# Output tiles in turn over four buffers and scaled x over six, in a linear-attention and FFN kernel

## The chip, the cores and the metric

The kernel runs on one core of a Trainium2 chip. The metric is the device time of one execution in microseconds (us); the lower, the better. A core has five engines that this text names as the profile does: PE (matrix multiplication, with its weight loads, PEld, beside it), DVE (VectorE), ACT (ScalarE), POOL (GpSimd) and SP (SyncE, which here only issues transfers). They run side by side, each in the order of its own instructions, and wait for each other through semaphores.

## The reference

Eight batches, eight heads, 576 tokens, head size 64. Every row of q and k is mapped to 256 positive features, and the attention is linear: keys and values are summed first, and each query is multiplied with the sum.

```python
def phi(x):
    proj = np.einsum('bhsd,df->bhsf', x, w_phi)                  # 64 -> 128
    proj = proj - np.max(np.abs(proj), axis=-1, keepdims=True)
    return np.concatenate([np.exp(proj), np.exp(-proj)], axis=-1)
q_p, k_p = phi(q), phi(k)
kv = np.einsum('bhsf,bhsd->bhfd', k_p, v)
num = np.einsum('bhsf,bhfd->bhsd', q_p, kv)
den = np.einsum('bhsf,bhf->bhs', q_p, np.sum(k_p, axis=2))[..., None] + 1e-06
x = (num / den)                      # reordered to 4608 tokens x 512
out = (np.maximum(x @ w_gate, 0.0) * (x @ w_val)) @ w_out        # 512 -> 1536 -> 512
```

The outputs are 4608 x 512 numbers in float32.

## The kernel before

**Stages.** For a batch, k and q are loaded, turned (so that the head dimension lies along the partitions) and multiplied with w_phi; DVE takes the largest absolute value of each row (`row_max`, L319), ACT the exponentials (L368, L565), POOL scales v (L328). PE sums keys and values (L486, L509), a copy takes the sums out of PSUM (L422), and PE multiplies them with the queries (L595). DVE joins the two halves of the features (L614, L626), takes the reciprocal of the denominator (L633), and POOL multiplies with it (L635): the result is `xu`, 128 tokens of scaled x in bf16. In the first two batches (`TURN = 2`) PE turns `xu` (L648 to L657); from then on, and for the chunks that hold the last 64 tokens of two batches, SP issues a transposing transfer `xT<-xu` (L643). The flag `by_dma` says which of the two holds for a chunk.

**FFN.** `ffn(g)` is called for nine groups of 512 tokens: eight batches, and a ninth with the remaining tokens of all batches. A group has twelve steps of gate and value products (L725, four matmuls each), a copy of the value product (L740), a joint relu and product into `h2` (L747), and then four output tiles of 128 tokens: twelve matmuls (L773, three thirds of four) into one PSUM bank `po`, a copy of it by ACT or DVE into an SBUF tile `out_sb` (L787), and a transfer of 256 KB to HBM which SP issues (`store`, L754; the last group stores in two halves, one issued by SP and one by ACT, L758).

**Order.** `ORDER` (L26) is a list of 1427 numbered steps, written out by hand, that says in which order the steps of all batches and groups are issued; a prime at a number gives a copy to the other engine. Nothing reorders them later: each engine runs its instructions, and SP and POOL issue their transfers, in that order.

**Buffers.** A tile of a pool takes the next buffer of its name. Before an instruction may write a buffer again, it waits until all that read the buffer's tile before has ended, a transfer's landing included. So `out_sb`, with two buffers, waits for the landing of the store of the tile two before it, and `xu`, with three, for the transposing transfer of the tile three before it:

```python
x["xu"] = sb_f.tile([P, H, D], BF16, name="xu")                     # L634, pool sb_f: 3 buffers
out_sb = sb_g.tile([P, DM], FP32, name="out_sb", bufs=2)            # L785
```

PSUM has eight banks, taken in turn by all products (`bank()`, L176). PE may write a bank again when the copy or reduction that read it has ended, so a late copy of `po` holds up whatever PE writes eight banks later.

The q and k of the first two batches are turned by PE and copied into tiles `tT4` (1 KB a partition, three buffers) and `tT8` (2 KB a partition, two buffers) of the pool `sb_T` (`turned_copy`, L282). From batch 2 on a transfer turns them and these five buffers are not used any more.

Of the kernel before, what the change touches and what calls it, by code (L numbers as in the profile page):

```python
# [8 lines left out]
FP32 = mybir.dt.float32  # L9
BF16 = mybir.dt.bfloat16  # L10
# [5 lines left out]
TURN = 2  # L16
# [103 lines left out]
def kernel(  # L120
# [21 lines left out]
    B, H, S, D = q.shape  # L142
    F = w_phi.shape[1]
    DFF = moe_w_gate.shape[1]
    DM = out.shape[1]
    P = 128
# [373 lines left out]

    GROUPS = ((0, 3), (3, 3), (6, 2))

    def q_item(key, groups, T, chunks, by_dma, blocks=None):


# [57 lines left out]
        for ci, (batches, place, col, dst, xkey) in enumerate(chunks):  # L583
            x = xs[ci]
            np_ = P // len(batches)
            for j, (lo, n) in enumerate(GROUPS):

                @atoms.add("n", *key, ci, j)
                def _(alt, x=x, j=j, lo=lo, n=n, batches=batches, place=place):
                    for bi, b in enumerate(batches):  # L590
                        pn = x["pn", j, bi] = bank()
                        for i in range(n):
                            slot, blk = place(lo + i)
                            for s in range(2):
                                nc.tensor.matmul(  # L595
                                    pn[:, E * (2 * i + s) : E * (2 * i + s + 1)],
                                    lhsT=x["qp"][:, s, slot, blk, :],
                                    rhs=kv_of(b, lo + i)[:, s, :],
                                )

                def halves(x, j, lo, n, batches, np_=np_):
                    for bi in range(len(batches)):
                        rows = slice(np_ * bi, np_ * (bi + 1))
                        ab = x["pn", j, bi][:, 0 : 2 * E * n].rearrange(
                            "p (c s e) -> p c s e", s=2, e=E
                        )
                        yield rows, ab[rows]

                @atoms.add("nt", *key, ci, j)
                def _(alt, x=x, j=j, lo=lo, n=n, batches=batches, col=col, np_=np_, halves=halves):  # L610
                    x["t", j] = sb_s.tile([P, 3, E], FP32, name="t", bufs=4)
                    for rows, ab in halves(x, j, lo, n, batches):
                        c = st["c"][rows, col(lo) : col(lo + n - 1) + 1 : col(1) - col(0)]
                        nc.vector.tensor_tensor(  # L614
                            x["t", j][rows, 0:n],
                            ab[:, :, 1],
                            c[:, :, None].to_broadcast([np_, n, E]),
                            op=ALU.mult,
                        )

                @atoms.add("nu", *key, ci, j)
                def _(alt, x=x, j=j, lo=lo, n=n, batches=batches, halves=halves):
                    if "u" not in x:
                        x["u"] = sb_f.tile([P, H, E], FP32, name="u")
                    for rows, ab in halves(x, j, lo, n, batches):
                        nc.vector.tensor_tensor(  # L626
                            x["u"][rows, lo : lo + n], ab[:, :, 0], x["t", j][rows, 0:n], op=ALU.add
                        )

            @atoms.add("xu", *key, ci)  # L630
            def _(alt, x=x):
                x["r"] = sb_s.tile([P, H, 1], FP32, name="r")
                nc.vector.reciprocal(x["r"], x["u"][:, :, D : D + 1])  # L633
                x["xu"] = sb_f.tile([P, H, D], BF16, name="xu")  # L634
                copy_of(alt, nc.gpsimd, nc.vector).tensor_tensor(  # L635
                    x["xu"], x["u"][:, :, 0:D], x["r"].to_broadcast([P, H, D]), op=ALU.mult
                )

            if by_dma:

                @atoms.add("xd", *xkey)
                def _(alt, x=x, dst=dst):
                    nc.sync.dma_start_transpose(out=dst(), in_=x["xu"].rearrange("p h d -> p (h d)"))  # L643

            else:

                @atoms.add("xT", *xkey)
                def _(alt, x=x):  # L648
                    x["pt"] = turn_on_pe(
                        [x["xu"][:, 2 * i : 2 * i + 2].rearrange("p a d -> p (a d)") for i in range(NDC)]  # L650
                    )

                @atoms.add("xc", *xkey)
                def _(alt, x=x, dst=dst):
                    copy_by(copy_of(alt, "DVE", "ACT"))(
                        dst(), x["pt"][:, 0 : NDC * P].rearrange("p (a b) -> p a b", b=P)
                    )  # L657
# [55 lines left out]
            q_tails(b // 2)  # L713


    def ffn(g):
        st = {}
        steps = [(fi, 0, SF) for fi in range(NFC)]
        if g == 0:
            steps = [(fi, P * lo, P * hi) for lo, hi, f0, f1 in FIRST for fi in range(f0, f1)]  # L720

        def half_step(fi, w, lo, hi):
            ps = bank()[:, 0 : hi - lo]
            for dc in range(NDC):
                nc.tensor.matmul(  # L725
                    ps,
                    lhsT=w[:, dc, P * fi : P * fi + P],
                    rhs=xTs[g][:, dc, lo:hi],
                    start=(dc == 0),
                    stop=(dc == NDC - 1),  # L730
                )
            return ps

        for n, (fi, lo, hi) in enumerate(steps):

            @atoms.add("fv", g, n)
            def _(alt, n=n, fi=fi, lo=lo, hi=hi):
                ps = half_step(fi, wv_sb, lo, hi)
                st["val", n] = sb_g.tile([P, SF], BF16, name="val_sb")[:, 0 : hi - lo]
                copy_by(copy_of(alt, "ACT", "DVE"))(st["val", n], ps)  # L740

            @atoms.add("fg", g, n)
            def _(alt, n=n, fi=fi, lo=lo, hi=hi):
                if "h2" not in st:
                    st["h2"] = sb_h.tile([P, NFC, SF], BF16, name="h2")
                ps = half_step(fi, wg_sb, lo, hi)
                nc.vector.scalar_tensor_tensor(  # L747
                    st["h2"][:, fi, lo:hi], ps, 0.0, st["val", n], op0=ALU.max, op1=ALU.mult
                )

        def store(t, out_sb, c0, c1):
            if g < B:
                rows = out[S * g : S * g + SF, c0:c1].rearrange("(p c) n -> c p n", c=C)
                nc.sync.dma_start(out=rows[t], in_=out_sb)  # L754
                return
            for half, eng in enumerate((nc.sync, nc.scalar)):
                r0 = S * (2 * t + half) + SF
                eng.dma_start(  # L758
                    out=out[r0 : r0 + SM, c0:c1], in_=out_sb[SM * half : SM * (half + 1), :]
                )  # L760

        for t in range(4):
            cols = LAST if g == B and t == 3 else ((0, DM),)
            for part, (c0, c1) in enumerate(cols):
                for third in range(3):

                    @atoms.add("fo", g, t, part, third)
                    def _(alt, t=t, part=part, third=third, c0=c0, c1=c1):
                        if third == 0:
                            st["po", t, part] = bank()[:, 0 : c1 - c0]  # L770
                        po = st["po", t, part]
                        for fi in range(4 * third, 4 * third + 4):
                            nc.tensor.matmul(  # L773
                                po,
                                lhsT=st["h2"][:, fi, P * t : P * t + P],
                                rhs=wo_sb[:, fi, c0:c1],
                                start=(fi == 0),
                                stop=(fi == NFC - 1),
                            )
                        if third < 2:  # L780
                            return
                        if part:
                            out_sb = sb_f.tile([P, H, E], FP32, name="u").rearrange("p h e -> p (h e)")
                        else:
                            out_sb = sb_g.tile([P, DM], FP32, name="out_sb", bufs=2)  # L785
                        out_sb = out_sb[:, 0 : c1 - c0]
                        copy_by(copy_of(alt, "ACT", "DVE"))(out_sb, po)  # L787
                        store(t, out_sb, c0, c1)

    for g in range(B + 1):  # L790
        ffn(g)
# [54 lines left out]
```

## Time and profile before

| | us |
|---|---|
| Median of 3 runs | 379.87 |
| The runs | 379.75, 379.87, 386.1 |
| The profiled execution: its own time | 382.8 |
| Its span, first to last instruction | 380.8 |
| PE busy in the span | 365.3 (96%) |
| DVE busy | 290.4 (76%) |
| ACT busy | 213.6 (56%) |
| POOL busy | 151.2 (40%) |

The profiled execution took 2.0 us more than its span, which is what lies around the first and the last instruction, and 2.9 us more than the median. TensorE's granted clock was full in all 40 slices. Times within the execution are counted from the start of the span. A row of the timeline gives start, duration, engine, line, operation, tiles and count, and in brackets how long the engine stood idle before and what ended that.

### The profile page before, as it was taken

How to read it: one execution, taken by the hardware profiler on the slowest of the kernel's cores; microseconds unless marked ns; L12 is line 12 of the kernel's file. 1: busy time of each engine (PE TensorE's matmuls, PEld its weight loads, DVE VectorE, ACT ScalarE, POOL GpSimd, SP SyncE). 2: the span in 40 equal slices, each digit the busy share in tenths (PEclk: the TensorE clock that was granted, in tenths of full speed). 3: DMA queues.
4: the chain of work that ended last, by engine and by line, in shares of the span. 5: the costliest groups of instructions: out<-in, count | busy, mean ns of one | idle time of the engine just before them, and what ended most of it. 6: DMA issues, size and time to landing. Idle time of an engine off the chain costs nothing.

```text
span 380.8 us, 8916 instructions
## 1 busy us (share of the span) xinstructions
PE 365.3 (96%) x3452; PEld 196.8 (52%) x3502; DVE 290.4 (76%) x633; ACT 213.6 (56%) x509; POOL 151.2 (40%) x201
## 2 busy tenths in 40 slices
PE   7789999898999999999989999999999999999996
PEld 4467455445555545464545544465455444444443
DVE  6998989797886789888858886988768927834641
ACT  6997888776776556885864549882750212111101
POOL 5882663359265283911752035933710220010000
PEclk9999999999999999999999999999999999999999
DMA  8999999999199959880378768720410131011003
GB/s 258 204 200 218 228 143 143 199 239 118 36 208 228 161 87 167 164 183 14 72 126 197 108 162 126 144 16 16 109 58 2 28 87 53 3 53 71 2 0 110
DMA packets 87929, 45.10 MB, mean 118 GB/s; under 512 B 55824, under 2 KB 82000, under 8 KB 87888
## 3 DMA queue, kind: packets, MB, share of 16 engines
q1 hardware_dynamic: 60208, 30.42, 36.4%
q0 software_dynamic: 27200, 13.57, 28.2%
q10 hardware_dynamic: 480, 0.56, 0.5%
q8 instruction: 27, 0.44, 0.5%
q14 instruction: 14, 0.11, 0.1%
HBM read 37.78 MB, written 9.44 MB: 124 GB/s over the span
## 4 chain that ended last, share of the span: by engine, by line
PE 79%; ACT 8%; DMA 5%; POOL 2%; issue 2%; DVE 1%; SPq 1%; another core or an unknown queue 0%; DVEq 0%; POOLq 0%
PE pa L725 44%; PE pa L773 20%; PE pa L595 4%; PE pa L312 4%; PE pa L486 3%; ACT kp L368 3%; ACT qp L565 3%; DMA vn<-in_v_dram 3%; DMA out_dram<-out_sb 2%; PE pa L547 2%; POOL vs L328 1%; SPq L292 1%; PE pa L509 1%; PE pa L271 1%; DMA vn<-in_k_dram 1%
## 5 line engine op out<-in xcount | busy, mean ns | idle before, releaser
L725 PE MATMUL pa<-xT,wv_sb 128*128 128x512 bf16 (+1 forms) x384 | 97.9, 370 | 0.9
L725 PE MATMUL pa<-xT,wg_sb 128*128 128x512 bf16 (+1 forms) x385 | 98.0, 370 | 0.8
L773 PE MATMUL pa<-wo_sb,h 128*128 128x512 bf16 (+2 forms) x427 | 97.6, 373 | 1.1 <-issue 0.3
L747 DVE SCALAR_TENSOR_TENSOR h<-pa,val_sb 128x512 bf16<-128x512 f32 (+1 forms) x112 | 74.6, 669 | 26.8 <-PE pa L725 20.7
L740 ACT CAST val_sb<-pa 128x512 bf16<-128x512 f32 (+1 forms) x67 | 38.1, 575 | 97.9 <-PE pa L725 88.8
L635 POOL TENSOR_TENSOR xu<-u,r 128x512 bf16<-128x512 f32 x36 | 37.3, 1041 | 139.3 <-DVE r L633 69.7
L565 ACT ACTIVATE qp<-pa 128x512 bf16<-128x512 f32 x144 | 76.2, 616 | 14.4 <-PE pa L547 14.1
L368 ACT ACTIVATE kp<-pa 128x512 bf16<-128x512 f32 (+1 forms) x152 | 77.6, 603 | 11.8 <-PE pa L312 10.4
L328 POOL TENSOR_TENSOR vs<-vn,ek 128x512 bf16<-128x512 f32 (+1 forms) x68 | 67.4, 1004 | 34.4 <-DMA vn<-in_v_dram 18.0
L725 PEld LDWEIGHTS <-wv_sb 128*128 128x128 bf16 x448 | 41.8, 98 | 45.0 <-issue 1.2
L725 PEld LDWEIGHTS <-wg_sb 128*128 128x128 bf16 x448 | 41.6, 98 | 43.4 <-issue 0.5
L773 PEld LDWEIGHTS <-h 128*128 128x128 bf16 x444 | 40.8, 98 | 44.6 <-issue 0.8
L319 DVE TENSOR_REDUCE mq<-pa 128x4 f32<-128x512 f32 x72 | 46.5, 683 | 11.1 <-PE pa L312 11.0
L319 DVE TENSOR_REDUCE mk<-pa 128x4 f32<-128x512 f32 (+1 forms) x76 | 47.8, 654 | 3.9 <-ACT kp L368 2.3
L626 DVE TENSOR_TENSOR u<-pa,t 128x195 f32<-128x195 f32 (+3 forms) x120 | 38.1, 333 | 3.3
L614 DVE TENSOR_TENSOR t<-pa,cq 128x195 f32<-128x195 f32 (+3 forms) x120 | 36.9, 326 | 2.5 <-PE pa L595 1.3
L787 DVE COPY out_sb<-pa 128x512 f32<-128x512 f32 x21 | 14.5, 688 | 28.8 <-PE pa L773 20.3
L595 PEld LDWEIGHTS <-qp 128*128 128x128 bf16 x640 | 28.1, 98 | 14.2 <-ACT qp L565 0.9
L740 DVE CAST val_sb<-pa 128x512 bf16<-128x512 f32 (+1 forms) x45 | 30.7, 682 | 4.4 <-PE pa L725 3.0
L595 PE MATMUL pa<-kv,qp 128*128 128x65 bf16 x640 | 31.1, 193 | 1.1 <-ACT qp L565 0.5
L787 ACT COPY out_sb<-pa 128x512 f32<-128x512 f32 (+1 forms) x15 | 8.9, 594 | 23.5 <-PE pa L773 18.7
L486 PEld LDWEIGHTS <-kp 128*128 128x128 bf16 x480 | 16.7, 97 | 5.9 <-issue 1.5
(68 smaller groups left out, 262.7 us busy)
## 6 DMA issues: line engine op xcount, KB each, us to landing
out_dram<-out_sb SPq DMA_DIRECT2D x32, 256.0 KB, 2.9
vn<-in_v_dram SPq DMA_DIRECT2D x6, 1024.0 KB, 7.1
qn<-in_q_dram POOLq DMA_DIRECT2D x8, 512.0 KB, 8.5
kn<-in_k_dram POOLq DMA_DIRECT2D x6, 512.0 KB, 8.6
wv_sb<-in_moe_w_val_dram POOLq DMA_DIRECT2D x3, 512.0 KB, 10.4
wg_sb<-in_moe_w_gate_dram POOLq DMA_DIRECT2D x3, 512.0 KB, 9.1
wo_sb<-in_moe_w_out_dram POOLq DMA_DIRECT2D x1, 1536.0 KB, 19.9
vn<-in_v_dram SPq DMA_DIRECT2D x1, 1152.0 KB, 11.7
```

The source lines that it names most:

```text
L319: nc.vector.tensor_reduce(m, some.rearrange("p (c f) -> p c f", f=F), axis=AX.X, op=ALU.max, apply_absolute_value=True,)
L328: eng.tensor_tensor(dst[:, :, s, 0:D], src, ek[:, :, s : s + 1].to_broadcast(list(src.shape)), op=ALU.mult,)
L368: nc.scalar.activation(st["kp"][:, s, 0 : n // 2, par, :], st["banks"][par][:, 0 : n // 2 * F].rearrange("p (a f) -> p a f", f=F), AF.Exp, ...
L565: nc.scalar.activation(x["qp"][:, s, slot].rearrange("p a b -> p (a b)"), st["cols", i][par], AF.Exp, scale=sign,)
L595: nc.tensor.matmul(pn[:, E * (2 * i + s) : E * (2 * i + s + 1)], lhsT=x["qp"][:, s, slot, blk, :], rhs=kv_of(b, lo + i)[:, s, :],)
L614: nc.vector.tensor_tensor(x["t", j][rows, 0:n], ab[:, :, 1], c[:, :, None].to_broadcast([np_, n, E]), op=ALU.mult,)
L626: nc.vector.tensor_tensor(x["u"][rows, lo : lo + n], ab[:, :, 0], x["t", j][rows, 0:n], op=ALU.add)
L635: copy_of(alt, nc.gpsimd, nc.vector).tensor_tensor(x["xu"], x["u"][:, :, 0:D], x["r"].to_broadcast([P, H, D]), op=ALU.mult)
L725: nc.tensor.matmul(ps, lhsT=w[:, dc, P * fi : P * fi + P], rhs=xTs[g][:, dc, lo:hi], start=(dc == 0), stop=(dc == NDC - 1),)
L740: copy_by(copy_of(alt, "ACT", "DVE"))(st["val", n], ps)
L747: nc.vector.scalar_tensor_tensor(st["h2"][:, fi, lo:hi], ps, 0.0, st["val", n], op0=ALU.max, op1=ALU.mult)
L773: nc.tensor.matmul(po, lhsT=st["h2"][:, fi, P * t : P * t + P], rhs=wo_sb[:, fi, c0:c1], start=(fi == 0), stop=(fi == NFC - 1),)
```

## The change

The five buffers of `tT4` and `tT8` are used again once they are free.

- From group 2 on, every second output tile is a `tT8` tile read as float32, the others stay `out_sb`. The sizes are equal (2 KB a partition). The tiles take four buffers in turn, so a copy waits for the store of the tile four before it. Groups 0 and 1 keep the two buffers (`g < TURN`), and so does the small last piece, which goes into a tile named `u`.
- Of the scaled x that a transfer turns, every second tile is a `tT4` tile (1 KB a partition, as before), the others stay `xu`. That makes six buffers; a multiplication waits for the transposing transfer of the tile six before it.
- `ORDER` and all else are the same: no instruction, transfer or engine is added, removed or moved, no pool grows, and only the buffers and the waits that follow from them differ.

```diff
+    x_count = [0]
+
     def q_item(key, groups, T, chunks, by_dma, blocks=None):
...
-                x["xu"] = sb_f.tile([P, H, D], BF16, name="xu")
+                if by_dma and x_count[0] % 2:
+                    x["xu"] = sb_T.tile([P, 4, P], BF16, name="tT4", bufs=3)
+                    x["xu"] = x["xu"].rearrange("p a (b d) -> p (a b) d", d=D)
+                else:
+                    x["xu"] = sb_f.tile([P, H, D], BF16, name="xu")
+                x_count[0] += by_dma
                 copy_of(alt, nc.gpsimd, nc.vector).tensor_tensor(
...
+    t_count = [0]
+
     def ffn(g):
...
+        def out_tile():
+            if g < TURN or t_count[0] % 2:
+                t = sb_g.tile([P, DM], FP32, name="out_sb", bufs=2)
+            else:
+                t = sb_T.tile([P, 8, P], BF16, name="tT8", bufs=2)
+                t = t.rearrange("p a b -> p (a b)").bitcast(FP32)
+            t_count[0] += 1
+            return t
...
                         else:
-                            out_sb = sb_g.tile([P, DM], FP32, name="out_sb", bufs=2)
+                            out_sb = out_tile()
```

The names of the tiles and of the semaphores tell what is different on an engine. On DVE, in group 3 (batch 3's outputs, at 194 to 201 us of the profile), the two copies of output tiles stand ahead of three row maxima. In the rows the words behind "waits" are semaphores: PE and DVE of those engines' own progress, DMAHW0 to DMAHW7 of eight lanes on which transfers report their landing in turn. Before:

```order
L422 CAST kv_4002<-pa_3981 128x260 [waits PE_49]
L787 COPY out_sb_4008<-pa_3945 128x512 [waits DMAHW2_49,DMAHW3_49,DMAHW1_49,DMAHW7_49,DMAHW0_49,PE_49]
L787 COPY out_sb_4029<-pa_4011 128x512 [waits DMAHW3_49,DVE_49,PE_49]
L319 TENSOR_REDUCE mq16_3849<-pa_4059 128x4 [waits PE_49]
L319 TENSOR_REDUCE mq16_3849<-pa_4060 128x4 [waits PE_49]
L319 TENSOR_REDUCE mq8_4081<-pa_4072 128x4 [waits PE_49]
L422 CAST kv_4116<-pa_4095 128x260 [waits PE_49]
```

The same place of DVE in the change:

```order
L422 CAST kv_4002<-pa_3981 128x260 [waits PE_49]
L805 COPY tT8_4008<-pa_3945 128x512 [waits DMAHW7_49,PE_49]
L805 COPY out_sb_4029<-pa_4011 128x512 [waits DMAHW2_49,DMAHW1_49,PE_49]
L319 TENSOR_REDUCE mq16_3849<-pa_4059 128x4 [waits PE_49]
L319 TENSOR_REDUCE mq16_3849<-pa_4060 128x4 [waits PE_49]
L319 TENSOR_REDUCE mq8_4081<-pa_4072 128x4 [waits PE_49]
L422 CAST kv_4116<-pa_4095 128x260 [waits PE_49]
```

Nothing moved. Before, the copy into `out_sb_4029` waits on lane 3 for the store of the tile `out_sb_3940`, two tiles back; in the change it waits on lane 1 for the store of `out_sb_3299`, four tiles back, and on lane 2 for a load of v that stood earlier on SP. On PE, at the same place, the next sums of keys and values follow eight banks after `pa_4011`, in before as in the change:

```order
L547 MATMUL pa_4085<-qT1_3131,w2_100 128x512 [waits Activation_49]
L547 LDWEIGHTS w2_100
L547 MATMUL pa_4086<-qT1_3131,w2_100 128x512 [waits Activation_49]
L486 LDWEIGHTS kp_3886 [waits DVE_49]
L486 MATMUL pa_4095<-vs_4083,kp_3886 128x65 [waits Pool_49]
```

The weight load of `kp_3886` carries the wait for the bank: it may go when DVE has ended its copy into `out_sb_4029`, which empties `pa_4011`.

## The prediction

> **What bounds the kernel now.** I read the page first (busy times, then the chain that ended last), then the windows from 100 us on, where the new buffers come into use, then the waits of every engine there, and last the timeline around the waits that the buffers cause.
>
> ```profile
> PE 365.3 (96%) x3452; PEld 196.8 (52%) x3502; DVE 290.4 (76%) x633; ACT 213.6 (56%) x509; POOL 151.2 (40%) x201
> PE 79%; ACT 8%; DMA 5%; POOL 2%; issue 2%; DVE 1%; SPq 1%; another core or an unknown queue 0%; DVEq 0%; POOLq 0%
> 100.00:199.67 99.67, 97.83 (x973) 52.62 (x985) 80.42 (x181) 66.87 (x157) 51.97 (x65) 1.00 0.77 137
> 199.67:377.10 177.43, 176.06 (x1308) 88.74 (x1332) 122.83 (x255) 66.09 (x149) 39.47 (x48) 1.00 0.32 70
> ```
>
> The first two rows say that PE is the bound: busy for 96% of the span, and 79% of the last chain. The last two are windows: length, then the busy time of PE, PEld, DVE, ACT and POOL. From 100 us to the last matmul PE stands idle for 99.67 - 97.83 = 1.84 us and 177.43 - 176.06 = 1.37 us, together 3.2 us. The change acts only in this part: groups 0 and 1 keep their two buffers, and where the windows begin the first scaled x is made that a transfer turns. Whatever a wait costs DVE, ACT, POOL or SP, the end moves only by what PE idles for it. So 3.2 us is the most that a removed wait can give, unless PE's work itself became shorter, and no instruction of PE is touched. Matmuls of this size run at their pace: the chain of waits has
>
> ```profile
> 302.92 0.86 PE pa L773 x4
> 330.48 5.18 PE pa L725 x24
> ```
>
> that is 0.86 / 4 = 0.215 and 5.18 / 24 = 0.216 us for one, at a granted clock of 1.00.
>
> **Which of the waits that go were waited for.** The list of waits (total, times, longest) over the whole span has these that bear on the buffers:
>
> ```profile
> DVE out_sb L787 <- DMA out_dram<-out_sb: 8.2, 3, 3.4
> POOL xu L635 <- DVE r L633: 69.7, 15, 17.8
> POOL xu L635 <- issue: 45.3, 5, 26.7
> PE pa L486 <- DVE out_sb L787: 0.9, 1, 0.9
> PE pa L271 <- DVE out_sb L787: 1.1, 1, 1.1
> ```
>
> Three copies of an output tile waited for a store, for 8.2 us in all; PE idled for such a copy twice. The timeline of DVE and PE shows the three, with what PE did about the second:
>
> ```profile
> 69.90 0.69 DVE L787 COPY out_sb<-pa 128x512 f32<-128x512 f32 x1 [1.73 <-DMA out_dram<-out_sb]
> 70.65 0.38 PE L271 MATMUL pa<-ident,xu 128*128 128x128 bf16 x4 [1.09 <-DVE out_sb L787]
> ...
> 191.73 8.24 SPq L754 DMA_DIRECT2D out_dram<-out_sb  x3
> 193.96 3.40 PE L773 MATMUL pa<-wo_sb,h 128*128 128x512 bf16 x15
> 195.48 0.25 POOL L414 CAST vs<-ek 128x16 bf16<-128x16 f32 x1
> 198.35 0.38 PE L547 MATMUL pa<-qT,w 64*128 64x512 bf16 x2
> 198.92 0.69 DVE L787 COPY out_sb<-pa 128x512 f32<-128x512 f32 x1 [3.43 <-DMA out_dram<-out_sb]
> 199.67 0.29 PE L486 MATMUL pa<-vs,kp 128*128 128x65 bf16 x4 [0.94 <-DVE out_sb L787]
> ...
> 312.52 0.69 DVE L787 COPY out_sb<-pa 128x512 f32<-128x512 f32 x1 [3.04 <-DMA out_dram<-out_sb]
> ```
>
> The chain of waits has at the second and the third:
>
> ```profile
> 191.73 7.07 DMA out_dram<-out_sb
> ...
> 304.33 7.23 PE pa L773 x33
> 311.61 2.32 PE pa L773 x10
> ```
>
> The first belongs to group 0, which the change leaves as it is (the 1.1 us of PE with it). At the third PE goes on without a pause: its matmuls run, by the last two rows, from 304.33 to 311.56 and from 311.61 to 313.93, and the copy came while the next tile was being added up. So that wait is worth nothing to PE, nor would the copy have come much sooner, since the matmuls of its own tile lie in the same stretch. There remains the second, in group 3.
>
> **The wait at 198.9 us, worked out.** The tile's twelve matmuls are the last of the 15 shown (one record of 16 is missing) and end at 193.96 + 3.40 = 197.36. The copy started only at 198.92, because the store of the tile two before it, issued at 191.73, landed at 198.80: the chain has it for 7.07 us. With four buffers the copy waits for the store of group 2's last tile, which was issued before the value and gate products of group 3, and starts when PE is done, at about 197.4. With its 0.69 us it ends at about 198.1 instead of 199.61. Behind it on DVE stand three row maxima and a copy of key-value sums, and behind it on SP the tile's own store; all may come up to 1.5 us sooner. PE's next product needs the bank that this copy empties. PE was done with what stands before that at 198.35 + 0.38 = 198.73, and the scaled v that it needs as well was ready at 195.48 + 0.25 = 195.73. So it starts at 198.73 instead of 199.67: 0.94 us of PE, not the 3.43 us of DVE and not the 7.07 us that the chain books on the store, because PE had work under the rest.
>
> What is late next? PE's following products need banks and data of DVE and ACT:
>
> ```profile
> 198.76 1.09 ACT L565 ACTIVATE qp<-pa 128x512 bf16<-128x512 f32 x2 [0.39 <-PE pa L547]
> 199.53 1.88 DVE L319 TENSOR_REDUCE mq<-pa 128x4 f32<-128x512 f32 x3
> 200.42 1.02 PE L725 MATMUL pa<-xT,wv_sb 128*128 128x512 bf16 x3
> 202.15 0.73 PE L595 MATMUL pa<-kv,qp 128*128 128x65 bf16 x18
> ```
>
> The value product at 200.42 writes the bank that the first row maximum empties; it would come at 199.48, and the maximum, 1.88 / 3 = 0.63 us long, can start behind the earlier copy and end by about 199.0. The products at 202.15 come at 201.21 and need the exponentials, which end at 199.85 with or without the change. Nothing there eats the 0.94 us. From there to the end PE idles only 1.37 us in all, so it is nearly always PE itself that sets its pace, and a gain made at 199 us arrives at the end.
>
> **Scaled x in six buffers: nothing.** POOL idles long before these multiplications, but not for a buffer:
>
> ```profile
> 133.74 1.04 POOL L635 TENSOR_TENSOR xu<-u,r 128x512 bf16<-128x512 f32 x1 [7.44 <-PE pa L725]
> 139.69 2.06 POOL L635 TENSOR_TENSOR xu<-u,r 128x512 bf16<-128x512 f32 x2
> 206.16 0.20 DVE L633 RECIPROCAL r<-u 128x8 f32<-128x8 f32 x1
> 206.50 1.04 POOL L635 TENSOR_TENSOR xu<-u,r 128x512 bf16<-128x512 f32 x1 [10.77 <-issue]
> 333.08 0.20 DVE L633 RECIPROCAL r<-u 128x8 f32<-128x8 f32 x1
> 333.42 1.04 POOL L635 TENSOR_TENSOR xu<-u,r 128x512 bf16<-128x512 f32 x1 [26.69 <-issue]
> DMA to landing us min/median/max: 2.4/2.6/7.2
> ```
>
> Where the list of waits names no releaser ("issue"), the reciprocal ended 0.14 us before (206.36 and 206.50, 333.28 and 333.42): the data came last. The tightest place is the second of the two at 139.69, whose buffer was written at 133.74, three tiles before; its transfer went out at about 134.8, and by the last row (the transfers out of xu) even the slowest landing, 7.2 us, would be 142.0, 1.3 us after that multiplication's start at 140.7. That is the upper bound; in the trace the two ran without a pause, so it is 0. SP and PE, which wait for xu, gain nothing either. Nor does any instruction pay for the new tiles: the sizes, the engines and the numbers of transfers are the same, and a wait of DVE or ACT for a store four tiles back ends before one for a store two tiles back.
>
> **The sum.** Against the profiled execution's 382.8 us (span 380.8, and 2.0 around it): 0 for the first wait, 0.94 for the second, 0 for the third, 0 for scaled x, hence 381.9. Its own time stands 2.9 us above the median of the runs; from the median the sum is 379.87 - 0.94 = 378.9 us.
>
> Both bounds of the 0.94 us hang on when the store of 191.73 lands in an execution.
>
> ```profile
> DMA to landing us min/median/max: 2.0/2.6/9.8
> q0 software_dynamic: 1040, 0.52, 45.9%
> q1 hardware_dynamic: 832, 0.66, 21.3%
> ```
>
> The first row is that of all output stores. If it lands within 197.36 - 191.73 = 5.63 us, the wait is not there to be removed, and the change gives 0. At 9.8 us it would land at 201.5, the bank would come free 2.7 us later than in the trace, and the change would give 0.94 + 2.73 = 3.7 us. I take the trace's own 7.07 us: the load that slows it (last rows: transfers from 190 to 200 us, where POOL's queue, q0, takes 45.9% of the 16 transfer engines with a load of k) stands in the same place of the order in every execution. The Trainium skill says ("DMA: Bandwidth & Descriptors", section "Queues, rings and completion order") that a transfer engine takes turns between the queues that have work, packet by packet. By that rule a store beside one other busy queue takes about twice the median of 2.6 us, 5.2 us as an estimate from that row, and the sum would be 379.9; the trace has 7.07 us, so the rule alone does not explain the wait.
>
> **The rivals.**
>
> *No gain, 379.9 us.* In executions without the profiler the store shares the transfer engines with the one load alone and lands after twice the median, 2 x 2.6 = 5.2 us, inside the 5.63 us, so that there is no wait to remove; or what PE gains at 199 us it loses at one of the small pauses behind. Against it: the trace shows 7.07 us at this place, and only 1.37 us of pauses follow. (The first of these is what the Trainium skill's page on DMA, named above, would make of it.)
>
> *More gain, 376.7 us.* Other waits for stores are near their edge in the trace and late in other executions, so that the change takes away all of PE's 3.2 us: 379.87 - 3.2. Against it: the list of waits has PE waiting for a copy of output only at the two places shown.
>
> *Slower, 382.3 us.* The store and what follows it on SP go out up to 1.5 us sooner, and transfers are bunched differently; the turned x that PE needs lands late. The tightest place behind:
>
> ```profile
> 200.06 0.39 SPq L214 DMA_DIRECT2D vn<-in_v_dram  x1
> 227.85 2.52 SPq L643 DMA_TRANSPOSE xT<-xu  x2
> 236.43 1.03 PE L725 MATMUL pa<-xT,wv_sb 128*128 128x512 bf16 x4
> ```
>
> The second of the two transposing transfers goes out at about 229.1; PE reads it at 236.43, and with the gain at 235.5. With the slowest landing of such a transfer, 7.2 us, it is there at 236.3 and costs 0.8 us, so the sum is 379.7; with the slowest of all stores, 9.8 us, it is there at 238.9, and PE loses 3.4 us: 378.9 + 3.4 = 382.3. It decides from a landing after 7.3 us on. Against it: the median is 2.6 us, and every transfer keeps its place in the order of SP and POOL.
>
> **How the numbers follow.** The forecast has 0.58, no gain 0.22, more gain 0.08, slower 0.12. The likeliest is 378.9 us. The lower end of the range, 377.0, takes in all but the last 0.3 us of the greater gain; the upper one, 381.1, lies halfway between no gain and the slower rival (379.9 and 382.3). Outside stay about half of each of these two cases, 0.10, and as much again for runs that scatter. All cases lie within 2% of 379.87 us (372.3 to 387.5), about what a measurement of this kernel can tell from no change. To leave it, a gain would have to be more than twice all of PE's idle time after 100 us, and a loss would have to be 7.6 us, some seven times the longest wait of PE for a copy of output shown above; one of the three runs, at 386.1, shows that times well above the median occur. So 0.02 for faster by over 2%, 0.95 within, 0.03 slower.
>
> **What would show it.** Right: the copy of group 3's last tile starts within 0.1 us of its matmuls, the product of keys and values behind it has no idle time, DVE's waits for stores shrink from 8.2 us to the 1.7 us of group 0, and POOL's waits before xu stay as long as they are, for the reciprocals. Wrong: that copy starts in time and PE then idles there for something else, a new wait appears at turned x or turned k, or POOL's multiplications start sooner.

## The result and the profile after

| | before | after |
|---|---|---|
| Median, us | 380.36 (22 runs, 379.37 to 386.1) | 379.21 (22 runs, 378.62 to 383.03) |
| Profiled execution, us | 382.8 | 378.75 |
| Its span, us | 380.8 | 376.9 |

After over before is 0.9957, with a 95% interval of 0.9937 to 0.9977: a gain of 0.9 to 2.4 us, and no difference by the bound of 2%. This ratio leaves out the run of 386.1 us, which is more than 1.5% above the fastest of its kernel, and is not that of the two medians, which would be 0.9970. The forecast of 378.9 us was 0.3 us too low, its 0.94 us of gain lies at the lower end of the interval, and the range held the time.

The page of after has these two rows for those that the prediction showed first (busy times, then the shares of the chain that ended last):

```profile
PE 367.3 (97%) x3502; PEld 196.5 (52%) x3502; DVE 290.6 (77%) x633; ACT 213.2 (57%) x509; POOL 151.5 (40%) x201
PE 93%; ACT 5%; DVE 1%; DMA 1%; issue 0%; DVEq 0%
```

PE's share of the chain went from 79% to 93%, that of transfers from 5% to 1%, and no store stands in it any more. Not all of that is the change: the chain of before also has a load of v, ahead of the part where the change acts, that took longer than the 7.07 us of the store:

```profile
70.41 9.53 DMA vn<-in_v_dram
```

The windows of after (length, busy time of PE, PEld, DVE, ACT, POOL, clock, share of the transfer engines, GB/s) are split at the place in group 3. The first begins where that of before begins, counted back from this place without the wait (99.67 - 0.94 = 98.73 us), and the second is as long as that of before:

```profile
97.09:195.82 98.73, 98.73 (x987) 52.64 (x985) 80.74 (x181) 65.98 (x156) 52.10 (x65) 1.00 0.80 138
195.82:373.25 177.43, 177.43 (x1334) 88.76 (x1332) 122.78 (x255) 66.97 (x150) 39.54 (x48) 1.00 0.32 70
```

PE is idle for 0.0 us in both, against 1.84 and 1.37 us in before. That fall of 3.2 us is not all gain. After has 3502 matmul records, before 3452, and 14 and 26 of the missing ones lie in these two windows (987 against 973, 1334 against 1308). The second windows are equally long, so all of their 1.37 us was matmuls whose records are missing; of the 1.84 us in the first, 0.94 us was the wait and 0.90 us missing records. That makes 2.3 us of what the prediction counted as idle time.

The timeline of after at the last tile of group 3:

```profile
188.84 0.53 SPq L772 DMA_DIRECT2D out_dram<-out_sb  x1
191.97 0.69 DVE L805 COPY tT<-pa 128x512 f32<-128x512 f32 x1 [0.17 <-PE pa L791]
194.56 0.69 DVE L805 COPY out_sb<-pa 128x512 f32<-128x512 f32 x1 [1.90 <-PE pa L791]
195.52 0.38 PE L549 MATMUL pa<-qT,w 64*128 64x512 bf16 x2
195.83 0.30 PE L486 MATMUL pa<-vs,kp 128*128 128x65 bf16 x4
196.58 1.02 PE L734 MATMUL pa<-xT,wv_sb 128*128 128x512 bf16 x4
```

The copy at 194.56 waits for the matmuls of its own tile (L791) and for nothing else; it was a store that ended its wait of 3.43 us in before. The sums of keys and values at 195.83 (L486) follow without idle time, where before had 0.94 us. The list of waits of after, for copies of output (L805) and scaled x (L642; `tT` are the added buffers):

```profile
ACT out_sb L805 <- PE pa L791: 16.3, 4, 8.9
DVE out_sb L805 <- PE pa L791: 13.6, 6, 4.4
DVE tT L805 <- PE pa L791: 11.7, 6, 4.5
ACT tT L805 <- PE pa L791: 7.0, 5, 2.9
...
POOL xu L642 <- DVE r L635: 53.5, 13, 13.7
POOL tT L642 <- DVE r L635: 40.9, 9, 17.8
POOL tT L642 <- issue: 32.1, 3, 26.7
```

Copies wait for matmuls only, not for stores. POOL waits in front of scaled x for the reciprocals (`r`), in the added buffers as in the old ones.

**Where the 3.9 us between the two spans lie.** All the traces hold the same number of PE's weight loads, so the same load can be found in two traces by counting, and the time from one to another compared. I cut the span at six of them; the heads give their times in after. In us:

| stage in after | 0 to 21.4 | to 65.1 | to 84.2 | to 90.3 | to 195.1 | to 202.3 | to 376.9 |
|---|---|---|---|---|---|---|---|
| before | 21.45 | 44.09 | 20.28 | 7.28 | 104.80 | 8.23 | 174.60 |
| after | 21.37 | 43.75 | 19.03 | 6.12 | 104.81 | 7.23 | 174.59 |

The place in group 3 lies in the stage to 202.3 us: 1.00 us. The other 2.83 us lie before 90.3 us, where the change does not act: start-up and small pauses, group 0's wait for a bank (the 1.09 us that the prediction showed at 70.65), and in before a late scaled v (`vs`, `vsm`), which the timeline of before has as

```profile
91.14 0.19 PE L486 MATMUL pa<-vsm,kp 128*128 128x65 bf16 x1 [0.56 <-POOL vsm L395]
...
92.08 0.28 PE L486 MATMUL pa<-vs,kp 128*128 128x65 bf16 x4 [0.29 <-POOL vs L328]
```

Whether these come is chance: the same program, profiled again, had neither (below). Everything behind, 279 us in two stages, agrees to 0.01 us.

### The profile page after: what moved, and what is told of

Read it like the earlier page. It is cut to its first block, busy times and chain, and to the rows that moved or that the text cites. A ratio compares the mean times of both kernels' runs of the same rounds, so it can differ in the third digit from the quotient of the medians.

```text
span 376.9 us, 8960 instructions
## 1 busy us (share of the span) xinstructions
PE 367.3 (97%) x3502; PEld 196.5 (52%) x3502; DVE 290.6 (77%) x633; ACT 213.2 (57%) x509; POOL 151.5 (40%) x201
## 4 chain that ended last, share of the span: by engine, by line
PE 93%; ACT 5%; DVE 1%; DMA 1%; issue 0%; DVEq 0%
PE pa L734 49%; PE pa L791 25%; PE pa L597 5%; PE pa L312 5%; PE pa L486 4%; PE pa L549 2%; ACT kp L368 2%; ACT qp L567 2%; PE pa L271 1%; PE pa L509 1%; DMA vn<-in_k_dram 1%; DVE tT L284 0%; ACT xT L662 0%; ACT kv L422 0%; ACT val_sb L749 0%
## 5 line engine op out<-in xcount | busy, mean ns | idle before, releaser
L791 PE MATMUL pa<-wo_sb,h 128*128 128x512 bf16 (+2 forms) x444 | 99.9, 373 | 0.0
L734 PE MATMUL pa<-xT,wv_sb 128*128 128x512 bf16 (+1 forms) x400 | 99.3, 370 | 0.1
L734 PE MATMUL pa<-xT,wg_sb 128*128 128x512 bf16 (+1 forms) x400 | 99.3, 370 | 0.0
L791 PEld LDWEIGHTS <-h 128*128 128x128 bf16 x444 | 40.8, 98 | 44.6 <-issue 0.8
L642 POOL TENSOR_TENSOR xu<-u,r 128x512 bf16<-128x512 f32 x22 | 22.9, 1042 | 67.1 <-DVE r L635 53.5
L642 POOL TENSOR_TENSOR tT<-u,r 128x512 bf16<-128x512 f32 x14 | 14.6, 1043 | 73.0 <-DVE r L635 40.9
L805 DVE COPY out_sb<-pa 128x512 f32<-128x512 f32 x14 | 9.6, 688 | 13.8 <-PE pa L791 13.6
L486 PEld LDWEIGHTS <-kp 128*128 128x128 bf16 x480 | 16.6, 98 | 3.9 <-issue 0.7
```

The lines of the kernel that those rows point to most:

```text
L642: copy_of(alt, nc.gpsimd, nc.vector).tensor_tensor(x["xu"], x["u"][:, :, 0:D], x["r"].to_broadcast([P, H, D]), op=ALU.mult)
L734: nc.tensor.matmul(ps, lhsT=w[:, dc, P * fi : P * fi + P], rhs=xTs[g][:, dc, lo:hi], start=(dc == 0), stop=(dc == NDC - 1),)
L791: nc.tensor.matmul(po, lhsT=st["h2"][:, fi, P * t : P * t + P], rhs=wo_sb[:, fi, c0:c1], start=(fi == 0), stop=(fi == NFC - 1),)
```

## The experiments

The theory: a single tile, the last of group 3, carries the gain. The store of the tile two before it lands late because POOL's load of k (the last one, for batch 7) shares the transfer engines with it; the copy, and with it the bank, come late; PE idles. Rivals: the gain is spread over many waits near their edge; it comes from scaled x; or the spans differ by chance alone. The table has all runs; "group 3" is the stage to 202.3 us as above minus the 7.22 us that it takes without a wait, and "landing" is how long the store two tiles before took from issue, by the row of transfers.

| kernel | median, us | ratio to before, 95% | group 3, us | landing, us |
|---|---|---|---|---|
| before, first profile | 380.36 | | 1.0 | 7.1 |
| before, second profile | | | 2.3 | 8.4 |
| before, third profile | | | 0.6 | 6.6 |
| after | 379.21 | 0.9957 (0.9937 to 0.9977) | 0.0 | 6.8 |
| only outputs in four | 379.70 | 0.9975 (0.9950 to 1.0001) | 0.0 | 6.6 |
| only scaled x in six | 380.55 | 0.9999 (0.9967 to 1.0031) | 4.0 | 8.5 |
| one tile | 379.37 | 0.9981 (0.9955 to 1.0007) | 0.0 | 6.8 |
| all but group 3 | 379.73 | 0.9979 (0.9954 to 1.0004) | 0.5 | 6.6 |
| every third tile in `tT8` | 379.17 | 0.9979 (0.9969 to 0.9990) | 0.0 | 8.4 |
| before, short load of k | 380.26 | 1.0000 (0.9968 to 1.0032) | 0.0 | 2.5 |
| after, short load of k | 379.38 | 0.9987 (0.9956 to 1.0017) | 0.0 | 2.5 |
| after, group 0 in three | 379.39 | 0.9971 (0.9941 to 1.0002) | 0.0 | 6.7 |
| one buffer | 396.31 | 1.0420 (1.0368 to 1.0471) | 3.3 | |

The times alone separate little: of the kernels but that with one buffer, only after and "every third tile in `tT8`" have an interval that leaves out 1, and the intervals of one tile (0.9981) and of all but group 3 (0.9979) hold the theory and the rival both. Each ratio is to runs of before taken along with that kernel, whose medians were 380.09 to 380.29 us. What is said below on the place of the gain rests on the profiled executions, one of each kernel and three of before. The traces separate more, since the stage to 195.1 us is 104.81 us and that to the end 174.6 us (174.57 to 174.61) in every kernel but that with one buffer; only group 3's stage differs.

**Only the outputs in four buffers**, scaled x in three as before:

```diff
-                if by_dma and x_count[0] % 2:
+                if False:
```

> The output tiles in four buffers, scaled x in its three as before. Theory (PE gains only where it waited for the bank behind group 3's last tile): as fast as the whole change, ratio 0.9957 to the kernel before or 1.0 to 1.6 us less, and in the profile no wait of DVE for a store after group 0. Rival (six buffers for scaled x carry part of it): less gain than the whole change, under 1 us.

Measured: 379.70 us, and no idle time in group 3. In the trace the outputs are the half of the change that acts.

**Only scaled x in six buffers**, outputs in two:

```diff
-            if g < TURN or t_count[0] % 2:
+            if True:
                 t = sb_g.tile([P, DM], FP32, name="out_sb", bufs=2)
```

> Scaled x in six buffers, the output tiles in two as before. Theory: no difference from the kernel before, ratio within 0.9985 to 1.0015, and DVE waits again for a store ahead of group 3's last tile, with about 0.9 us of idle PE behind it. Rival: 0.3 to 1 us less than before.

Measured: 380.55 us, no difference from before. The timeline of this kernel has the wait of before at the same place, and longer:

```profile
190.19 9.68 SPq L772 DMA_DIRECT2D out_dram<-out_sb  x3
...
196.87 0.38 PE L549 MATMUL pa<-qT,w 64*128 64x512 bf16 x2
198.82 0.69 DVE L805 COPY out_sb<-pa 128x512 f32<-128x512 f32 x1 [4.80 <-DMA out_dram<-out_sb]
199.56 0.30 PE L486 MATMUL pa<-vs,kp 128*128 128x65 bf16 x4 [2.32 <-DVE out_sb L805]
...
201.42 1.91 PE L734 MATMUL pa<-xT,wg_sb 128*128 128x512 bf16 x4
```

The store of 190.19 landed after 8.5 us, and PE idled 2.32 us. The last row shows that it did not end there: four matmuls that take 1.02 us elsewhere took 1.91. The windows of this kernel have the granted clock as the third number from the end:

```profile
200.00:201.00 1.00, 0.95 (x19) 0.61 (x17) 1.00 (x3) 0.00 (x0) 0.00 (x0) 0.96 0.60 190
201.00:204.00 3.00, 3.00 (x22) 1.62 (x21) 1.39 (x4) 1.57 (x3) 0.00 (x0) 0.50 0.75 183
204.00:205.00 1.00, 1.00 (x10) 0.57 (x8) 1.00 (x4) 0.00 (x0) 0.00 (x0) 0.84 1.04 358
```

0.04 x 1 + 0.50 x 3 + 0.16 x 1 = 1.70 us of PE's time is lost to the clock. With the idle time that is 2.32 + 1.70 = 4.0 us, which is what the stage lost.

**One tile alone**: the last of group 3 (the sixteenth of the tiles) gets a buffer of its own, all others the two of before, scaled x three:

```diff
-            if g < TURN or t_count[0] % 2:
+            if t_count[0] != 15:
```

> One output tile alone, the last of group 3, takes a buffer of its own; all others stay in the two, and scaled x in its three. Theory: this one tile carries the whole gain, 0.94 us by the profile of before, ratio 0.9975 or lower. Rival (waits for stores elsewhere, which the profiled execution met in time, are late in other executions and carry the rest of the 1.6 us): half of the gain of the four buffers or less.

Measured: 379.37 us. The timeline of this kernel:

```profile
193.60 4.12 SPq L772 DMA_DIRECT2D out_dram<-out_sb  x2
...
199.27 0.69 DVE L805 COPY tT<-pa 128x512 f32<-128x512 f32 x1 [1.90 <-PE pa L791]
...
200.54 0.30 PE L486 MATMUL pa<-vs,kp 128*128 128x65 bf16 x4
```

The store of 193.60 landed after 6.8 us, at 200.4, when the copy that would have waited for it had long begun. The stage takes its 7.22 us. In the trace one tile gives all that the whole change gives.

**All but group 3**: the whole change, but group 3 keeps its two buffers:

```diff
-            if g < TURN or t_count[0] % 2:
+            if g < TURN or g == 3 or t_count[0] % 2:
```

> The whole change, but group 3's four output tiles stay in the two buffers of the kernel before. Theory: the gain is gone, ratio 0.9985 to 1.0015, and the profile has the wait of group 3 with 0.9 us of idle PE. Rival (spread over many tiles and executions): 0.5 us or more of gain stays.

Measured: 379.73 us, and in the trace the wait of group 3 is there again with 0.5 us, the smallest of the five executions that have it:

```profile
197.21 0.69 DVE L805 COPY out_sb<-pa 128x512 f32<-128x512 f32 x1 [2.89 <-PE pa L312]
...
197.95 0.30 PE L486 MATMUL pa<-vs,kp 128*128 128x65 bf16 x4 [0.40 <-DVE out_sb L805]
```

No other stage is longer or shorter than after's behind 90.3 us, so none of the other groups carries gain in this execution. The releaser in the first row is the one that came last by the profile, a reading to be careful with: L312 has nothing to do with this tile, and the store (issued at 190.50, landed after 6.6 us, at 197.1) ended 0.1 us before the copy. The time by itself doesn't tell this kernel from after or from before.

**Short load of k.** The load that POOL issues just ahead of the store is cut to the first of the eight heads; batch 7 works on batch 6's k in the other seven. Once in before, and once in after:

```diff
     def load_k(b):
+        if b == B - 1:
+            t = inputs["kn", b] = inputs["kn", b - 1]
+            nc.gpsimd.dma_start(out=t[:, 0:1], in_=main_rows(k, b, slice(0, 1)))
+            return
```

> The kernel before, two buffers, with the load of batch 7's k cut to its first head (64 KB instead of 512 KB; batch 7 works on batch 6's k in the other heads). Theory (the store that group 3's last copy waits for is late because POOL's load of k runs beside it): the store lands within 5.6 us instead of 7, the copy starts with its matmuls, PE has no idle time there, and the time falls as with four buffers, 1 to 1.6 us under before. Rival (the turning transfer of x that SP issues just ahead, or SP's queue itself, delays the store): it still takes about 7 us, and the wait stays.

> The whole change with the same cut load of batch 7's k. Theory: the wait is cured once already, so the second cure adds nothing: the same time as the whole change and as the run with the cut load alone, within 0.5 us. Rival (the two cure different losses): 1 us less than either.

Measured: 380.26 and 379.38 us. The timeline of the first, with two buffers as in before:

```profile
187.80 0.62 POOL L230 DMA_DIRECT2D kn<-in_k_dram  x1
...
189.17 6.71 SPq L758 DMA_DIRECT2D out_dram<-out_sb  x3
...
194.83 0.69 DVE L791 COPY out_sb<-pa 128x512 f32<-128x512 f32 x1 [1.90 <-PE pa L777]
```

and its transfers from 189 to 190 us (KB, us from issue to landing):

```profile
out_dram<-out_sb SPq DMA_DIRECT2D x1, 256.0 KB, 2.5
```

The same store, in the same place, landed after 2.5 us instead of 6.6 to 8.5, the copy waited for its matmuls only, and group 3 lost nothing, with two buffers. So it is the load of k that makes this store late. Whether it does so directly is not told apart: the turning transfer that SP issues between the two landed sooner as well, after 3.2 us instead of 6.6 to 7.2. In the timed runs the expected gain of 1 to 1.6 us does not show: the interval, 0.9968 to 1.0032, allows at most 1.2 us. The runs scatter from 378.91 to 386.34 us, and why was not profiled; that part stays open. With four buffers and the short load, group 3's stage is as long as with either alone, so the two cure the same loss; the 0.9 us between the two medians is within the intervals.

**Every third tile in `tT8`**, the others in `out_sb`, scaled x in three:

```diff
-            if g < TURN or t_count[0] % 2:
+            if g < TURN or t_count[0] % 3:
```

> Output tiles from group 2 on over three buffers (every third is a tT8 tile), scaled x in three as before. The last tile of group 3 then waits for the store of its group's first tile, which goes out about 5 us sooner than the one that it waited for. Theory (one tile, one tile further back is enough): no idle time of PE at the sums of keys and values in group 3, 0.0 us against after there; 1.0 to 1.6 us below before, so about 379 us, ratio 0.996. Rival (it takes all four buffers): the copy still waits and PE idles 0.3 us or more there.

Measured: 379.17 us, 0.9979 (0.9969 to 0.9990), a gain of 0.4 to 1.2 us. The timeline of this kernel:

```profile
185.70 0.34 SPq L772 DMA_DIRECT2D out_dram<-tT  x1
...
189.29 4.13 SPq L772 DMA_DIRECT2D out_dram<-out_sb  x2
...
194.95 0.69 DVE L805 COPY tT<-pa 128x512 f32<-128x512 f32 x1 [1.90 <-PE pa L791]
...
196.22 0.30 PE L486 MATMUL pa<-vs,kp 128*128 128x65 bf16 x4
```

The store of 189.29 was among the latest of all, 8.4 us, and cost nothing. But this kernel does not test what its expectation says. `tT8` still has two buffers, so four are in use: a tile in `out_sb` waits for the store three tiles back, and a tile in `tT8` for that six tiles back. The last tile of group 3 is one of the latter (`tT` in the row of 194.95), and does not wait for the store of its group's first tile. That one tile further back would be enough is an estimate from the first row: that store went out at 185.70, landed after 2.0 us, at 187.7, and so 7 us before the copy. Three buffers were not run.

**Before, profiled twice more**, unchanged:

> The kernel before, unchanged, profiled once more, to see how far the wait at group 3's last tile differs between executions of one program. Theory (the store beside the load of k lands 6.6 to 8.5 us after its issue in every execution): PE idles there between 0.4 and 4 us. Rival (the profiled wait was chance): in this execution PE does not idle there.

> The kernel before once more, as a further execution of the same program. Theory: PE idles 0.4 to 4 us at group 3's last tile, and every stretch between there and 100 us and behind it agrees with the others to 0.1 us. Rival: no idle time there.

Measured: 381.13 and 380.39 us. The timeline of the second profile of before:

```profile
188.85 9.54 SPq L754 DMA_DIRECT2D out_dram<-out_sb  x3
...
197.33 0.69 DVE L787 COPY out_sb<-pa 128x512 f32<-128x512 f32 x1 [4.72 <-DMA out_dram<-out_sb]
...
198.08 0.30 PE L486 MATMUL pa<-vs,kp 128*128 128x65 bf16 x4 [2.23 <-DVE out_sb L787]
```

and of the third:

```profile
189.86 7.79 SPq L754 DMA_DIRECT2D out_dram<-out_sb  x3
...
196.61 0.69 DVE L787 COPY out_sb<-pa 128x512 f32<-128x512 f32 x1 [2.98 <-DMA out_dram<-out_sb]
...
197.36 0.30 PE L486 MATMUL pa<-vs,kp 128*128 128x65 bf16 x4 [0.49 <-DVE out_sb L787]
```

The wait is there in each of the five profiled executions with two buffers in group 3 and the whole load of k: 0.5, 0.6, 1.0, 2.3 and 4.0 us, 1.7 us in the mean. Neither of these two executions had group 0's wait or the late scaled v. Behind 65 us they differ from after at group 3 alone.

**Group 0 in three buffers**: the whole change, and group 0's second tile goes into a buffer that later holds batch 3's turned q:

```diff
-            if g < TURN or t_count[0] % 2:
+            if t_count[0] == 1:
+                t = sb_in.tile([P, H * C // 2, P], BF16, name="qT1")[:, 0:8]
+                t = t.rearrange("p a b -> p (a b)").bitcast(FP32)
+            elif g < TURN or t_count[0] % 2:
```

> The whole change, and group 0's second output tile in a tile of batch 3's turned q that is not yet in use, so that group 0 has three buffers. Theory: it removes the other place where PE waited for a copy of output (1.1 us at 70 us in the profile of before, absent in the profile of the whole change): 0 to 1.1 us less than the whole change, which is a ratio of 0.994 to 0.9957 to before, and in the profile no idle PE at that place. Rival (what stands behind on SP takes the time again): the same as the whole change.

Measured: 379.39 us, not to be told from after. In its profiled execution, which took 385.06 us, no copy of group 0 waits for a store, but the timeline has another wait near the place:

```profile
68.07 0.40 PE L312 MATMUL pa<-w,kmT 64*128 64x128 bf16 x8 [0.88 <-DMA kmT<-km]
```

In the twelve profiles with two buffers in group 0 its wait is there twice (in the first of before and in one tile: a stage to 84.2 us of 20.3 us, against 19.0 to 19.1 in the other ten), so that there is seldom anything to gain here. The run doesn't decide more than that.

**One buffer** for the output tiles of groups 2 to 8:

```diff
-            if g < TURN or t_count[0] % 2:
+            if g >= TURN and "one" in kept:
+                return kept["one"]
+            if g < TURN:
...
+            if g >= TURN:
+                kept["one"] = t
```

> Output tiles of groups 2 to 8 in one buffer instead of two or four; scaled x in three as before. Each copy waits for the store of the tile just before it. Theory: where stores are quick (2.4 us, from group 5 on) PE goes on with the next tile and hardly idles; in group 3 three copies in a row come late, and PE stands before their banks for 4 us or more beyond what it lost in before; 3 to 8 us slower than before, ratio 1.008 to 1.02, and the idle time of PE lies in groups 2 to 4. Rival (copies in time matter in every group): over 10 us slower, with idle PE in all groups.

Measured: 396.31 us, a loss of 3.7% to 4.7%, and far more than the theory gave. The traces put the span 15.6 us behind after's: 0.5 us ahead of 65 us (chance), 3.9 in group 2, 3.3 in group 3, 3.2 in group 4, 1.3 in group 5, 0.1 from there to the last matmul, and 3.4 behind it, where each copy waits for the store before it and nothing else is left to do. The rival's time held (over 10 us slower), but not its place: groups 6 to 8 lost next to nothing before the last matmul. The timeline of this kernel in group 2 and in the last group:

```profile
154.14 0.59 ACT L808 COPY tT<-pa 128x512 f32<-128x512 f32 x1 [3.72 <-DMA out_dram<-tT]
154.78 0.55 PE L312 MATMUL pa<-w,kT 64*128 64x128 bf16 x7 [2.05 <-ACT tT L808]
...
381.34 0.59 ACT L808 COPY tT<-pa 128x512 f32<-128x512 f32 x1 [9.97 <-DMA out_dram<-tT]
...
388.22 0.45 ACT L808 COPY tT<-pa 128x352 f32<-128x352 f32 x1 [6.29 <-DMA out_dram<-tT]
```

and its windows behind the first:

```profile
154.00:155.00 1.00, 0.22 (x6) 0.22 (x6) 0.00 (x0) 0.86 (x2) 0.00 (x0) 0.93 1.29 82
155.00:158.00 3.00, 3.00 (x14) 1.07 (x9) 1.59 (x3) 3.00 (x9) 2.11 (x3) 0.50 0.53 138
158.00:159.00 1.00, 1.00 (x5) 0.42 (x4) 0.34 (x1) 1.00 (x5) 1.00 (x2) 0.87 0.00 0
```

Of the 3.9 us in group 2, 2.05 are idle time, and 0.07 + 1.50 + 0.13 = 1.70 us are the clock again, which the theory did not have.

## Why the prediction was right, and where it was not

**PE bounds, and the end moves by what PE idles.** Right. The stage behind group 3 takes 174.6 us whatever is removed in front of it, so what PE gains at 199 us arrives at the end whole.

**The one wait out of three.** Right. One tile alone gives in the trace what the whole change gives; group 0's wait and scaled x add nothing.

**0.94 us of PE, not 3.43 of DVE nor 7.07 of the store.** Right for the execution that it was read from: the stage became 1.00 us shorter. As a size for the median it was low. The prediction took the trace's own landing of 7.07 us, since the load stands in the same place in every execution. The place is the same, but the landing is not: 6.6 to 8.5 us. The loss follows it: 0.5 us at 6.6, 1.0 at 7.1, 2.3 at 8.4, and 4.0 at 8.5, where the clock came in. The mean of 1.7 us lies inside the 0.9 to 2.4 us that the ratio gives; that the timed runs lose it at the same place is likely, but no trace of them shows it. The bounds, 0 and 3.7 us, held all but the 4.0, which had a term that the prediction didn't know.

**The bound for no wait.** 5.63 us of landing was the point at which DVE would not wait. PE had work left behind that: with a landing of 7.07 us it lost 0.94, so it loses nothing up to about 7.07 - 0.94 = 6.1 us, 0.5 us later. The rival of no gain was thus nearer than it was drawn: the smallest landing measured beside the whole load, 6.6 us, is 0.5 us above that point. It did not come in any of the five profiled executions. Nor did a landing of 5.2 us, the prediction's estimate by the rule of the Trainium skill ("DMA: Bandwidth & Descriptors", section "Queues, rings and completion order"): the store beside the load took 6.6 us or more, and beside an eighth of it 2.5.

**The third wait, worth nothing.** Right for PE, wrong in the reason beside it, that the copy would not come much sooner. It does, as the same copy in the timeline of after shows:

```profile
307.54 0.69 DVE L805 COPY tT<-pa 128x512 f32<-128x512 f32 x1 [1.90 <-PE pa L791]
```

It starts 307.54 - 195.83 = 111.71 us behind the sums of keys and values of group 3, against 312.52 - 199.67 = 112.85 us in before, so 1.14 us sooner. PE gained nothing by it: the stage that holds it took 174.60 us in before and takes 174.59 now.

**The rivals.** More gain, 376.7 us, took PE's 3.2 us of idle time for real; 2.3 of them were missing records, and the counts on the page's first row (3452 matmuls, 3502 weight loads) pointed at it. For the same reason the 1.37 us behind 199.67 us, which the prediction took for pauses, were none. Slower, 382.3 us, did not come: no transposing transfer is waited for by PE in after.

**The median.** The forecast stood on three runs with a median of 379.87 us; the 22 runs have 380.36. The sum from this is 379.4, and the measured 379.21 lies 0.2 us below it: too small a gain and too low a start made up for each other in part.

## What to carry to other kernels

A late store costs what the engine that bounds the kernel idles for it, not what the chain or the waiting engine books; find the last wait of that engine, and the work that it still had. Where that wait hangs on a transfer beside another queue's load, one trace gives one draw of it: profile the kernel before again before putting a size on it, and compare by stages between the same instructions, since the first 90 us alone scatter by more than the gain. Before taking a window's idle time as the most that can be won, see whether all of its matmul records are there.

## What the runs showed of the hardware

**A pause can cost twice.** In two executions a pause of PE (2.32 us, and 2.05 with one buffer) was followed by 3.4 us at a granted clock of 0.50, for 1.70 us more each time. After pauses of 2.22, 2.23 and 2.89 us in three others (one tile, the second profile of before, group 0 in three buffers) the clock stayed at 1.00:

```profile
93.01 0.19 PE L486 MATMUL pa<-vsm,kp 128*128 128x65 bf16 x1 [2.22 <-POOL vsm L395]
...
94.65 0.19 PE L486 MATMUL pa<-vsm,kp 128*128 128x65 bf16 x1 [2.89 <-POOL vsm L395]
```

So the length alone doesn't decide. The Trainium skill ("TensorE: Matmul & The Clock Gate", "Part 1: The HAM clock gate (the "warmup" mystery)") says that the clock is gated by activity in a free-running window of 3413 ns; 1.70 / 0.50 = 3.4 us agrees with that length, and the free-running window with the chance in it. Its condition, a whole idle window, does not agree: both pauses were shorter, and what of the activity around them counts was not tried.

The clock records in the traces say more. Within an execution every change of the clock lies a whole number of steps of 3.413 us from the others: with one buffer at 11.49, 154.85 (42 steps) and 158.26 us. Counted by such steps from each execution's own records, PE stood idle for 2.1 and 2.05 us of the step that ended with the drop (197.50 to 200.91 us with scaled x alone, 151.44 to 154.85 with one buffer). The other three pauses are cut by the end of a step or begin before one, and the most idle time in one step is 2.0, 1.9 and 1.8 us. These five cases fit a limit on the idle time within one step, between 2.0 and 2.05 us, but they don't prove one: at the start of executions, where PE runs smaller matmuls, drops came after steps with 1.6 to 1.7 us of idle time.

Part of the scatter at the start is the same. Three executions have 3.4 us at a clock of 0.50 there (from 16.59, 13.42 and 13.25 us: scaled x alone, all but group 3, and after with the short load), and two more reach the full clock only at 18.3 and 18.6 us (only outputs, group 0 in three), where the others have it from 9.0 to 11.9 us on. The stage to 21.4 us takes 22.7 to 23.4 us in these five, and 21.4 to 21.9 us in the other eight.

**A store beside a load of another queue** took 6.6 to 8.5 us for 256 KB, and 2.5 us with seven eighths of that load taken away (two executions).
